# Loading a quad's queries and keys with one transfer over 120 partitions instead of two over 60, with a new rule table

## The chip, the cores and the metric

The kernel runs on one core of a Trainium2 chip. The metric is the device time of one execution in microseconds (us); the time before is the median of three runs. A profile of one further execution is shown beside it; its times are those of that one execution.

## The reference, cut to what matters

Two attention layers A and B with the same input `x` (2048 tokens of 640 numbers) and different weights are mixed by a gate per token. Each has 32 heads of 20 numbers, and the tokens are cut into 4 segments of 512.

```python
q, k, v = x @ wq, x @ wk, x @ wv                  # per head 20 numbers
for s in range(4):                                # segments of 512 tokens
    logits = einsum("hqd,hkd->hqk", qs, ks) * scale + mask
    a_dot  = softmax(logits) @ vs
    a_mem  = (phi(qs) @ M) / (phi(qs) @ z + 1e-6)
    o      = g * a_mem + (1 - g) * a_dot          # g = sigmoid(beta), per head
    M, z   = M + phi(ks).T @ vs, z + phi(ks).sum()
out = gate * (oA @ woA) + (1 - gate) * (oB @ woB) # gate per token
```

The mask takes out the keys that stand after the query, so that about half of the scores of a segment count.

## The kernel before, in words

One pass over eight windows `t` (segment `t // 2` of layer `t % 2`). In each window the projections q, k and v are made for 128 rows of the weights at a time. A product is kept near fp32 by splitting both sides into a high and a low part and adding three of the four products (line 819 for all of them but the first two and the last). The high and low parts of q and k are written to DRAM tensors `qd` and `kd` (line 798), three rows for each number of a head: (high, low, high) for q and (high, high, low) for k, so that one multiply over 3 x 20 = 60 rows gives the three products at once.

**Quads.** Attention works on a quad: four heads, as two pairs beside each other along the free axis and two halves of the array along the partitions. There are 64 quads, 8 in each window. `load_quads` reads a quad back from `qd` and `kd` into one of four buffers `qst` and one of four `kst` (line 1240): each is 128 partitions of 2 x 512 numbers, and half 0 has its 60 rows at partitions 0 to 59, half 1 at 64 to 123. That takes four transfers of 240 KB, two for q and two for k. A buffer is free when the quad four before it has had its second pass of scores (`t_over`).

**Two passes of scores.** `s_unit` multiplies q by k (line 1284) to find each query's largest score; VectorE takes the maximum out of PSUM with the triangle mask (line 1269), and the maxima `mx` are split in two parts, turned (line 1315), copied to a tile `mr` (line 1310) and sent by DMA into two spare rows of `qst` (line 1327). The matching rows of `kst` hold -1, so that `t_unit`, which multiplies k by q over 62 rows (line 1376), gives scores less their maximum. ScalarE takes the exponential into `p` (line 1368), GpSimd clears the half that is masked (line 1369), and `pv_unit` multiplies `p` with v (line 1396). The results go to DRAM tensors `dots`, come back (line 1517), are weighed by the inverse denominators (lines 1508 and 1509), turned, split (lines 1499, 1501 and 1502) and multiplied with `wo`, whose mixed form `wmix` is read through the buffers `wst` (line 567), as the other weights are. The memory `M` is updated in line 1030 and read in line 930.

**What sets the order.** The whole order is made when the kernel is built: a planner holds a clock for each half of TensorE and for each engine ("A", "D", "G" for ScalarE, VectorE, GpSimd, and "S" for SyncE, which issues all DMAs), with a cost in microseconds for each piece of work, and records the instructions in the order in which its model would do them. `dma(us, ...)` queues a transfer of `us` on a model of the DMA engines with at most 8 in flight. `put("D", 0.24, ...)` queues 0.24 us on VectorE; `anyof` gives a piece of work to the engine with the least queued. For each quad, a line of `RULES` sets in which order first ("S") and second ("T") passes stand, how they spread over the quad's time, and when work that may come late is let in. On the chip each engine takes its instructions strictly in the recorded order.

Of the kernel before, what the change touches and what calls it, by code (L numbers as in the profile page):

```python
# [42 lines left out]
def tile_gated_mix_infini_attn(  # L43
# [47 lines left out]
        0: "TTSSTTSSTS 1.01 2.38 0.22 8 0 1.6 1",  # L91
        1: "STTSTSSTST 1.021 2.38 0.4 4 0 1.6 1",
        2: "STSTSTSTST 0.96 2.38 0.3 8 0 1.6 1",
        3: "TTSTSTSTSS 0.967 2.38 0.33 8 0 2.23 1",
        4: "TTSSTTSSTS 1.028 2.22 0.3 8 0 1.6 1",
        5: "STSTSTSTST 1.01 2.38 0.38 8 0 2.37 1.15",
        6: "STTSTSSTST 1.01 2.38 0.3 8 0 1.6 1",
        7: "TSTTSSTSTS 0.96 2.11 0.27 8 0 1.6 1",
        8: "SSTSTSTSTT 1.013 1.26 0.3 8 0 1.6 1",
        9: "STTSTSSTST 1.01 2.38 0.28 8 0 1.6 1.33",  # L100
        10: "STTSTSSTST 1.01 2.38 0.3 8 0 1.6 1",
        11: "TSSTTSSTTS 1.077 1.88 0.3 8 0 1.6 1",
        12: "TSSTTSSTTS 1.01 2.38 0.3 8 0 2.97 1",
        13: "STTSTSSTST 1.01 1.86 0.23 8 0 1.31 0.39",
        14: "TSTSTSTSTS 1.01 2.38 0.3 8 0 1.6 1",
        15: "TTTSSTSTSS 1.01 2.38 0.3 8 0 1.6 1",
        16: "TTTSTSTSSS 0.996 2.38 0.3 8 0 1.6 1",
        17: "TTSTSTSTSS 1.01 3.27 0.3 8 0 1.6 1",
        18: "TTTSTSTSSS 1.01 2.38 0.3 8 0 1.6 1",
        19: "STSTSTSTST 1.01 2.38 0.32 8 0 1.6 1",  # L110
        20: "TSTSTSTSTS 1.01 2.38 0.28 0 0 1.6 1",
        21: "TSTSTSTSTS 0.985 2.38 0.3 8 3.8 1.6 1",
        22: "STSTSTSTST 1.013 2.38 0.37 0 1.4 1.6 1",
        23: "TSTSTSTSTS 1.01 2.38 0.3 4 0 1.6 1",
        24: "TSTSTSTSTS 1.065 2.38 0.36 8 0 1.8 1.23",
        25: "TTSSTTSSTS 1.01 2.38 0.3 8 0 1.6 1.84",
        26: "STSTTSTSTS 1.01 1.41 0.24 8 0 1.6 0.35",
        27: "SSTSTSTSTT 1.01 3.14 0.3 8 0 1.6 1",
        28: "TSTSTSTSTS 0.97 2.38 0.3 2 0 1.6 1",
        29: "TSTSTSTSTS 1.01 2.38 0.38 8 0 1.6 1",  # L120
        30: "STSTSTSTST 1.005 1.99 0.39 10 0 2.01 1.44",
        31: "TSTTSSTSTS 1.01 2.38 0.3 8 0 1.6 1",
        32: "SSTSTSTSTT 1.01 2.38 0.3 8 0 1.6 1",
        33: "TTTSSTSTSS 1.01 2.38 0.3 8 0 1.6 1",
        34: "TSTSTSTSTS 1.01 2.38 0.3 8 0 1.6 1",
# [1738 lines left out]
```

## Time and profile before the change

| what | before |
|---|---|
| median of 3 runs | 981.89 us (981.54 to 986.23) |
| the profiled execution, its own time | 985.52 us |
| its span, first to last instruction | 983.8 us |
| VectorE busy | 718.6 us (73%) |
| ScalarE busy | 671.4 us (68%) |
| GpSimd busy | 622.0 us (63%) |
| DMA moved | 236.02 MB, mean 240 GB/s |
| issues of 240 KB for `qst` and `kst` | 128 and 128 |

The busy share of an engine is an average over the whole span. For a multiply the profile shows when the array worked on anything at all: while one half of the array multiplies and the other waits, TensorE still counts as busy, so its share cannot show such a loss. "DMA share" in a window is the mean busy share of the 16 DMA engines; since packets overlap the window's ends it can stand a little over 1. "The chain" is the chain of work that ended last, followed back from the last instruction to what released each step; the releasers are inferred.

### The profile page before, as it was taken

The page shows a single profiled execution, that of the slowest core. Times are in us where ns is not written, and L with a number is a line of the kernel's source. Part 1 is how long each engine was busy: PE and PEld are TensorE (multiplying, and loading weights), DVE is VectorE, ACT ScalarE, POOL GpSimd, SP SyncE. Part 2 cuts the span into 40 slices and gives each one's busy share as a digit, 9 for nine tenths or more (in the row PEclk, how much of TensorE's full clock was granted, in tenths as well). Part 3 has the DMA queues.
Part 4 walks back from the last instruction along what each step waited for, and adds up shares of the span by engine and source line. Part 5 has one row for each costly group of instructions (what it writes and reads, how often), then busy time and mean ns, then how long its engine had stood idle before and what let it go on. Part 6 is the DMA issues. An engine that isn't in the chain of part 4 may idle for free.

```text
span 983.8 us, 31697 instructions
## 1 busy us (share of the span) xinstructions
PE 970.6 (99%) x11559; PEld 823.3 (84%) x11559; DVE 718.6 (73%) x2629; ACT 671.4 (68%) x1425; POOL 622.0 (63%) x1167
## 2 busy tenths in 40 slices
PE   9999999999999999999999999999999999999998
PEld 6987888888888888889788988797788888888876
DVE  4687966667788875887677968758666788678864
ACT  4378667677876676767686657876676667677572
POOL 4357558576557765767665677677584576658662
PEclk9999999999999999999999999999999999999999
DMA  6998988978888876887779777888675988779441
GB/s 212 306 314 233 304 256 300 311 225 253 261 288 236 296 223 189 297 259 232 208 219 286 233 222 221 236 276 249 201 229 175 283 263 265 233 228 275 115 128 54
DMA packets 148469, 236.02 MB, mean 240 GB/s; under 512 B 13173, under 2 KB 48794, under 8 KB 147994
## 3 DMA queue, kind: packets, MB, share of 16 engines
q1 hardware_dynamic: 148314, 234.00, 77.1%
q8 instruction: 91, 1.49, 0.7%
q14 instruction: 64, 0.52, 0.2%
HBM read 144.35 MB, written 95.11 MB: 243 GB/s over the span
## 4 chain that ended last, share of the span: by engine, by line
PE 91%; DMA 5%; issue 1%; DVE 1%; ACT 1%; SPq 1%; POOL 0%; ACTq 0%; POOLq 0%
PE bank L819 52%; PE bank L1396 15%; PE bank L1284 9%; PE bank L1376 8%; PE bank L930 3%; PE bank L972 2%; DMA wst<-in_a_wk_dram 2%; PE bank L1030 1%; DMA qst<-qd 1%; DMA kd<-row 1%; PE bank L869 1%; DMA kst<-kd 1%; DMA row<-dots 1%; PE bank L1211 0%; POOL wl L556 0%
## 5 line engine op out<-in xcount | busy, mean ns | idle before, releaser
L819 PE MATMUL bank<-row,wh 64*128 64x512 f32 x2308 | 479.5, 399 | 0.1
L1368 ACT ACTIVATE p<-bank 128x512 f32<-128x512 f32 x538 | 293.8, 601 | 101.9 <-PE bank L1376 84.6
L1269 DVE CUSTOM_DVE_ANT_0 junk<-bank,tri 128x128 bf16<-128x128 f32 (+2 forms) x768 | 279.5, 420 | 76.5 <-PE bank L1284 58.1
L819 PEld LDWEIGHTS bank<-row,wh 64*128 64x128 f32 x2308 | 315.8, 186 | 14.5 <-PE bank L819 1.1
L819 PE MATMUL bank<-row,wl 64*128 64x512 f32 x1154 | 293.6, 396 | 0.0
L1369 POOL TENSOR_SCALAR_AFFINE_SELECT p<-p 128x256 f32<-128x256 f32 (+1 forms) x538 | 195.0, 374 | 154.2 <-ACT p L1368 142.5
L556 POOL TENSOR_TENSOR wl<-wst,wh 128x640 fp32r<-128x640 f32 x115 | 180.4, 1574 | 64.7 <-ACT wh L558 46.0
L1269 DVE CUSTOM_DVE_ANT_0 bank<-bank,tri 128x512 f32<-128x512 f32 x256 | 172.6, 710 | 44.3 <-PE bank L1284 38.6
L819 PEld LDWEIGHTS bank<-row,wl 64*128 64x128 f32 x1154 | 176.4, 186 | 6.9 <-issue 0.8
L1284 PE MATMUL bank<-kst,qst 60*128 60x128 f32 (+3 forms) x1024 | 179.0, 329 | 2.4 <-ACT row L1499 1.3
L819 PE MATMUL bank<-wvh,row 64*128 64x320 f32 (+1 forms) x1280 | 172.8, 311 | 0.0
L1376 PE MATMUL bank<-qst,kst 62*128 62x128 f32 (+3 forms) x1024 | 170.4, 316 | 1.2 <-DVE row L1575 1.0
L819 PEld LDWEIGHTS bank<-wvh,row 64*128 64x128 f32 x1280 | 147.1, 186 | 2.2 <-PE bank L819 0.7
L1284 PEld LDWEIGHTS bank<-kst,qst 60*128 60x128 f32 x1024 | 129.0, 186 | 11.4 <-issue 2.0
L1376 PEld LDWEIGHTS bank<-qst,kst 62*128 62x128 f32 x1024 | 128.4, 186 | 10.9 <-issue 2.4
L1396 PE MATMUL bank<-p,vst 128*32 128x128 f32 (+3 forms) x1788 | 136.7, 425 | 0.0
L1396 PEld LDWEIGHTS bank<-p,vst 128*32 128x32 f32 x1788 | 55.6, 110 | 78.4 <-issue 55.7
L558 ACT CAST wh<-wst 128x640 fp32r<-128x640 f32 x119 | 86.1, 732 | 29.4 <-PE bank L819 14.0
L819 PE MATMUL bank<-wvl,row 64*128 64x320 f32 (+1 forms) x640 | 101.4, 310 | 0.0
L1269 DVE DVE_READ_ACCUMULATOR2_ANT mx<- 128x1 f32 x1024 | 100.0, 98 | 0.0
L819 PEld LDWEIGHTS bank<-wvl,row 64*128 64x128 f32 x640 | 82.1, 186 | 0.6 <-issue 0.4
L531 POOL TENSOR_TENSOR wvl<-wst,wvh 128x640 fp32r<-128x640 f32 (+1 forms) x48 | 60.0, 1254 | 16.1 <-DMA wst<-in_a_wv_dram 8.3
(122 smaller groups left out, 1160.4 us busy)
## 6 DMA issues: line engine op xcount, KB each, us to landing
qst<-qd SPq DMA_DIRECT2D x128, 240.0 KB
kst<-kd SPq DMA_DIRECT2D x128, 240.0 KB
qd<-row SPq DMA_DIRECT2D x40, 512.0 KB
kd<-row SPq DMA_DIRECT2D x40, 512.0 KB
dots<-row SPq DMA_DIRECT2D x56, 256.0 KB
wst<-wmix SPq DMA_DIRECT2D x35, 320.0 KB
qd<-row SPq DMA_DIRECT2D x40, 256.0 KB
kd<-row SPq DMA_DIRECT2D x40, 256.0 KB
```

Source lines behind the costliest of these rows:

```text
L531: put("G", 0.77 * n, lambda: nc.gpsimd.tensor_tensor(out=wl[:, a:b, :VN], in0=w3, in1=r32(wh[:, a:b, :VN]), op=ALU.subtract), end, prio=4)
L556: put(lo_eng, lo_cost, lambda: lo.tensor_tensor(out=wl, in0=w3, in1=r32(wh), op=ALU.subtract), end, prio=3)
L558: put("A", 0.625, lambda: nc.scalar.copy(wh, w3), low, prio=6)
L819: return nc.tensor.matmul(bank_of, lhsT=w[ROWS[half]], rhs=x_[ROWS[half]], start=start, stop=stop)
L930: return nc.tensor.matmul(pm[:, a - h0:c - h0, :].rearrange("p h e -> p (h e)"), lhsT=r32(pqTs[t, m][ROWS[half], P * n:P * (n + 1)]), rhs= ...
L972: return nc.tensor.transpose(px[:, n, r], block(n)[r], ident[r, r])
L1269: nc.vector.tensor_tensor_reduce(out=sc[:, off:off + w] if w == L else junk[:, at_:at_ + w], in0=sc[:, off:off + w], in1=tri[:, L - w:], s ...
L1284: lane_ops[half].append((mm(w), lambda pair=pair, qb=qb, off=off, w=w, r=r, sc=sc: nc.tensor.matmul(sc[:, off:off + w], lhsT=q[r, pair, P ...
L1368: put("A", 0.483, lambda: nc.scalar.activation(pt, sc, AF.Exp, scale=SCALE), lambda: (bank.give(sc), put("G", 0.15 + 0.105 * len(todo), la ...
L1369: "G", 0.15 + 0.105 * len(todo), lambda: nc.gpsimd.affine_select(out=blocks, in_=blocks, pattern=[[0, len(todo)], [1, P]], base=0, channel ...
L1376: lane_ops[half].append((mm(w), lambda pair=pair, kb=kb, off=off, w=w, r=r, sc=sc: nc.tensor.matmul(sc[:, off:off + w], lhsT=k[r, pair, P ...
L1396: nc.tensor.matmul(po[32 * j:32 * j + 32, P * kb:], lhsT=vst[t % 2][:, kb, h * E1:h * E1 + 32], rhs=pts[i, n, f][0][:, off:off + w], start ...
```

## The change

The rows of half 0 move from partitions 0 to 59 to partitions 4 to 63, so that with half 1 at 64 to 123 a quad fills 120 neighbouring partitions, and one transfer of 480 KB brings q and one k. Partitions 0 to 3 of `qst` then take part in the first pass for half 0 (64 rows instead of 60): they must be zero there, since the same partitions of `kst` hold -1. A DRAM tensor `zeros` is filled once from the cleared `qst[0]`, and a third transfer for each quad copies 16 KB of it over those four partitions. The maxima of half 0 now go to partitions 0 and 1, those of half 1 to 124 and 125, and the second pass takes partitions 0 to 63 and 64 to 125. The planner's costs change with it: 1.35 for a transfer of 480 KB instead of 0.95 for one of 240 KB, 0.05 for the zeros, 0.69 or 0.62 for the maxima of a unit instead of 0.763 or 0.638, and 0.14 instead of 0.24 for the turn. All 66 lines of `RULES` are new.

```diff
     RULES = {
-        0: "TTSSTTSSTS 1.01 2.38 0.22 8 0 1.6 1",
+        0: "TSTSTSTSTS 1.01 2.38 0.29 8 0 0.91 1",
...
+    zeros = dram.tile([4, 2, L], F32, name="zeros")
...
-        while next_load[0] < 64:
+        while next_load[0] < 64 and zeros_there:
...
-            done = then_all(4, lambda i=i: loaded.add(i))
-            r0, soon = 80 * u, marks[i - LEAD] if i >= LEAD else -2
+            done = then_all(3, lambda i=i: loaded.add(i))
+            r0, soon, lat = 80 * u, marks[i - LEAD] if i >= LEAD else -2, 0.9 if i > 1 else 2.8
             for dst, src in ((q, qd[t]), (k, kd[t])):
-                rows = src[r0:r0 + 80, :, :].rearrange("(p f d) c n -> f (d c) p n", p=2, f=2)
-                for half in range(2):
-                    dma(0.95, lambda dst=dst, src=rows[half], half=half: nc.sync.dma_start(
-                        out=r32(dst[64 * half:64 * half + 3 * DH, :, :]), in_=r32(src)), done, prio=soon, lat=0.9 if i > 1 else 2.8)
+                rows = src[r0:r0 + 80, :, :].rearrange("(p f d) c n -> (f d c) p n", p=2, f=2)
+                dma(1.35, lambda dst=dst, src=rows: nc.sync.dma_start(
+                    out=r32(dst[4:4 + 6 * DH, :, :]), in_=r32(src)), done, prio=soon, lat=lat)
+            dma(0.05, lambda q=q: nc.sync.dma_start(out=r32(q[:4, :, :]), in_=zeros), done, prio=soon, lat=lat)
...
-            r = slice(64 * half, 64 * half + 60)
+            r = slice(64, 124) if half else slice(0, 64)
...
-                put("D", sum(P * (qb + 1) for _, qb, _ in todo) / 960.0 + 0.125 * len(todo) - 0.02, both,
+                put("D", 0.69 if len(todo) > 1 else 0.62, both,
...
-        put("D", 0.24, lambda: turn_rows(i), lambda: mr_store.want(1, lambda mr: move_rows(i, mr), prio=0), prio=1)
+        put("D", 0.14, lambda: turn_rows(i), lambda: mr_store.want(1, lambda mr: move_rows(i, mr), prio=0), prio=1)
...
-            r = 64 * half + 60
+            r = 124 * half
...
-            r = slice(64 * half, 64 * half + 62)
+            r = slice(64, 126) if half else slice(0, 64)
...
+    at(9.0, lambda: dma(0.05, lambda: nc.sync.dma_start(
+        out=zeros, in_=r32(qst[0][:4, :1, :]).to_broadcast([4, 2, L])), lambda: (zeros_there.append(1), load_quads()), prio=-3))
```

What this moves on the engines is seen in the recorded order. A row is one instruction: line, operation, what it writes, what it reads, the shape written, and how many of the same follow each other. Line numbers of the code behind the new tensor are mostly one higher after the change.

SyncE's queue at the load of the first quad (`qst_80`, `kst_84`), before:

```order
L567 DMA wst_150<-in_a_wq_dram 128x640
L567 DMA wst_151<-in_a_wk_dram 128x640
L1240 DMA qst_80<-qd_97 60x2x512 x2
L1240 DMA kst_84<-kd_105 60x2x512 x2
L798 DMA qd_97<-row_249_384 128x2x512
L798 DMA qd_97<-row_250_385 128x512
```

and after:

```order
L568 DMA wst_152<-in_a_wk_dram 128x640
L1240 DMA qst_80<-qd_97 120x2x512
L1240 DMA kst_84<-kd_105 120x2x512
L1242 DMA qst_80<-zeros 4x1024
L799 DMA qd_97<-row_252_386 128x2x512
L799 DMA qd_97<-row_253_387 128x512
```

Four transfers have become three, at the same place between the weights and the next writes to `qd`.

SyncE's queue at the load of quad 11 (`qst_83`, `kst_87` out of `qd_98` and `kd_106`), in the second window, before; `inv` holds the inverse denominators and `dots` the results of a window:

```order
L1442 DMA dots_118<-row_3034_2944 128x512
L798 DMA kd_106<-row_3025_2937 128x2x512
L798 DMA kd_106<-row_3026_2938 128x512
L1465 DMA row_2826_2766<-inv_124 128x1x512
L1517 DMA row_3057_2969<-dots_117 128x1x512
L567 DMA wst_151<-wmix_137 128x5x128
L567 DMA wst_150<-wmix_137 128x5x128
L1240 DMA qst_83<-qd_98 60x2x512 x2
L1240 DMA kst_87<-kd_106 60x2x512 x2
L1240 DMA qst_80<-qd_98 60x2x512 x2
L1240 DMA kst_84<-kd_106 60x2x512 x2
```

and after:

```order
L1328 DMA qst_80<-mr_168 2x8x128 x2
L1443 DMA dots_117<-row_2456_2496 128x512
L1240 DMA qst_83<-qd_98 120x2x512
L1240 DMA kst_87<-kd_106 120x2x512
L1242 DMA qst_83<-zeros 4x1024
L539 DMA wst_151<-in_b_wv_dram 128x320
L799 DMA kd_106<-row_2572_2596 128x2x512
L799 DMA kd_106<-row_2573_2597 128x512
L568 DMA wst_150<-in_a_wk_dram 128x640
L1328 DMA qst_81<-mr_168 2x8x128 x2
```

Before, this load stood behind the way back of the first window's results and the mixed weights, with the next quad's load right behind it; after, it stands ahead of the last value weights of its window, ahead of all of those.

TensorE's queue ahead of the first quad's first scores, before:

```order
L819 MATMUL bank_144<-wvh,row_72_230 128x322
L819 MATMUL bank_141<-wvh,row_67_227 128x322
L819 MATMUL bank_144<-wvl,row_13_200 128x322
L819 MATMUL bank_141<-wvh,row_72_230 128x322
L819 MATMUL bank_144<-wvl,row_20_202 128x322
L819 MATMUL bank_141<-wvl,row_13_200 128x322
L819 MATMUL bank_144<-wvl,row_25_204 128x322
L1284 MATMUL bank_143<-kst_84,qst_80 128x512
```

and after:

```order
L820 MATMUL bank_142<-wvh,row_25_205 128x322
L820 MATMUL bank_145<-wvh,row_25_205 128x322
L820 MATMUL bank_142<-wvh,row_67_227 128x322
L820 MATMUL bank_145<-wvh,row_67_227 128x322
L820 MATMUL bank_142<-wvh,row_72_230 128x322
L1285 MATMUL bank_146<-kst_84,qst_80 128x512
```

The first scores are asked for earlier: 214 rows of the order stand ahead of them before, 200 after, and the low parts (`wvl`) of these two banks of the value product have moved behind them or far ahead. Over the whole program TensorE has the same multiplies in both; VectorE has 7 more of the subtractions and products over a whole row that `anyof` hands out (lines 1501 and 1508 before: 12 and 18, after the change 15 and 22), GpSimd 7 fewer (lines 1502 and 1509 before: 23 and 17, after 20 and 13).

More of the change, by code (lines that the diff above doesn't have):

```diff
@@ L1220, in quad @@
         return t, u, qst[i % NQ], kst[i % NQ]
-    loaded, next_load, t_over = set(), [0], set()
+    loaded, next_load, t_over, zeros_there = set(), [0], set(), []
     def load_quads():
-        while next_load[0] < 64:
+        while next_load[0] < 64 and zeros_there:
             i = next_load[0]
```

130 rows, old and new, of the table RULES are left out of this document.

## The prediction

> **What bounds the kernel now.** I read the head of the page and the shares of the chain first.
>
> ```profile
> span 983.8 us, 31697 instructions
> PE 970.6 (99%) x11559; PEld 823.3 (84%) x11559; DVE 718.6 (73%) x2629; ACT 671.4 (68%) x1425; POOL 622.0 (63%) x1167
> PE 91%; DMA 5%; issue 1%; DVE 1%; ACT 1%; SPq 1%; POOL 0%; ACTq 0%; POOLq 0%
> q1 hardware_dynamic: 148314, 234.00, 77.1%
> ```
>
> TensorE works 970.6 of 983.8 us, so it stands still for 13.2 us in all, and 91% of the chain is its own work. No other engine is full. The only other resource with a share worth a look is the DMA engines: 77.1% of their time, and 5% of the chain, about 49 us. Next the long pieces of the chain, in order of time (start, length, what), without those of TensorE:
>
> ```profile
> 21.11 9.61 DMA qst<-qd
> 30.78 8.25 DMA wst<-in_a_wk_dram
> 41.32 7.61 DMA wst<-in_a_wk_dram
> 175.35 6.69 DMA kst<-kd
> 658.92 5.19 DMA row<-dots
> 672.19 6.76 DMA kd<-row
> 704.18 2.28 issue
> ```
>
> Two of the pieces are loads of a quad, the thing that is changed: the first at 21 us, and one at 175 us. Then the busy times by window (start:end, length, then TensorE, its weight loads, VectorE, ScalarE, GpSimd with their counts, the granted clock, the DMA share and GB/s):
>
> ```profile
> 0.00:60.00 60.00, 57.07 (x482) 49.19 (x484) 37.26 (x122) 30.78 (x69) 25.34 (x46) 1.00 0.85 273
> 170.00:172.00 2.00, 2.00 (x30) 1.97 (x28) 0.00 (x0) 0.70 (x2) 1.85 (x2) 1.00 1.05 405
> 175.00:182.00 7.00, 7.00 (x75) 7.00 (x73) 5.26 (x5) 3.77 (x7) 4.71 (x3) 1.00 1.03 261
> 182.00:186.00 4.00, 2.67 (x21) 2.04 (x19) 2.59 (x5) 3.19 (x8) 2.47 (x3) 1.00 1.07 227
> 182.00:188.00 6.00, 4.67 (x38) 4.04 (x36) 4.59 (x7) 4.80 (x10) 4.07 (x6) 1.00 1.09 250
> 300.00:655.00 355.00, 354.64 (x4328) 302.15 (x4322) 267.44 (x951) 251.17 (x529) 239.73 (x434) 1.00 0.79 243
> 909.00:912.00 3.00, 3.00 (x45) 2.02 (x38) 2.50 (x9) 2.65 (x7) 3.00 (x4) 1.00 1.00 222
> 914.20:915.20 1.00, 1.00 (x19) 1.00 (x17) 0.96 (x5) 0.81 (x2) 0.82 (x4) 1.00 0.00 0
> ```
>
> The clock is 1.00 throughout. At 170 to 172 us, where transfers over 128 partitions run, full DMA engines move 405 GB/s. At 182 to 188 and at 909 to 912, with little in flight but loads of quads, engines that are just as busy move 250 and 222. So a load over 60 partitions keeps the engines busy for longer than its bytes need. That is the room this change has. How much of it is on the path is another matter, and the waits of TensorE (waiting line, what released it, us in total, times, longest) with the rows of its first scores in time order show it:
>
> ```profile
> PE bank L1284 <- ACT row L1499: 1.3, 1, 1.3
> PE bank L1376 <- DVE row L1575: 1.0, 1, 1.0
> PE bank L1284 <- ACT p L1368: 0.8, 1, 0.8
> 185.17 0.60 PE L1284 MATMUL bank<-kst,qst 60*128 60x512 f32 x2 [1.33 <-ACT row L1499]
> L1284 PE MATMUL bank<-kst,qst x176: 217/370/494, 32.9 to 158.1; 60*128 60x512 f32 x44, 60*128 60x128 f32 x44, 60*128 60x384 f32 x44, 60*128 60x256 f32 x44
> L1284 PE MATMUL bank<-kst,qst x992: 217/382/502, 32.9 to 921.6; 60*128 60x128 f32 x52, 60*128 60x512 f32 x51, 60*128 60x256 f32 x49, 60*128 60x384 f32 x47
> 926.99 0.65 PE L1284 MATMUL bank<-kst,qst 60*128 60x512 f32 x2
> 173.74 1.11 SPq L1240 DMA_DIRECT2D qst<-qd  x2
> 906.32 0.80 SPq L1240 DMA_DIRECT2D qst<-qd  x2
> ```
>
> A quad has 16 first-pass multiplies, so the 176 before 185 us are those of quads 0 to 10, and the one at 185.17 opens quad 11, whose load was issued at 173.74. TensorE stood still for 1.33 us ahead of it, and the DMA engines were full all the way. The 992 before 926.95 us are quads 0 to 61: quad 62 opens at 926.99, its load was issued at 906.32, and at 914.2 the DMA engines are empty. This load was there some 12 us too early. Both kinds exist, and a faster load is worth something in the first kind only.
>
> **The loads themselves.** A quad is 4 x 240 KB, 0.983 MB. At 250 GB/s that is 3.9 us, at 222 it is 4.4, at 405 it is 2.4. The trace has no load over 120 partitions: its bounds are 3.9 us (no faster) and 2.4 us (as fast as the row at 170 us). I take 2.7, since 120 neighbouring partitions are nearer to 128 than to 60. That saves 1.2 us for each quad and 77 us of DMA time over 64, and takes the DMA share from 77% to about 69%. On the path:
> - Around quad 11, 21 multiplies run in the 4 us from 182 against 75 in the 7 us before, which is 5.3 for each us against 10.7: half the work is missing, 2.0 us. The recorded order also puts this load ahead of the way back of the first window. I count **-2.0**; between 0 and -3.
> - In the first 60 us TensorE stands still for 2.9 us, of which the start of the program is the greater part, while the chain runs through three DMAs (9.61, 8.25 and 7.61 us). Three quads' loads, each 1.2 us shorter, bring what queues behind them 1 to 3.6 us forward; the value products of the window cover most of that. **-1.5**; between 0 and -4.
> - At 659 and 672 us the chain goes through `dots` and `kd`, and TensorE stands still 1.0 and 0.8 us there. Transfers that share the engines with shorter loads land sooner: **-0.5**; between 0 and -2.
> - The other loads are hidden as quad 62's is: **0**.
>
> [...]
>
> **What is added.** SyncE issues three transfers for a quad where it issued four.
>
> ```profile
> L1240 SPq DMA_DIRECT2D qst<-qd x128: 319/396/2036, 20.7 to 918.6; - x128
> L1240 SPq DMA_DIRECT2D kst<-kd x128: 315/417/1748, 22.4 to 919.6; - x128
> L1327 SPq DMA_DIRECT2D qst<-mr x128: 610/622/1134, 43.6 to 952.0; - x128
> SPq L1240 <- PE bank L1376: 76.3, 31, 8.2
> ```
>
> At some 0.4 us an issue (the middle number is the median in ns) the 64 fewer issues free 26 us of SyncE. It waits in other places: 76.3 us in all for the second pass that frees a buffer. So **0**; between -2 and 0. The zeros are 64 x 16 KB, 1 MB beside 236, nothing as bytes. But S now has to wait for them, and they are issued last. The nearest row is the small transfer of the maxima, 0.62 us of issue. Where the load has 12 us to spare this is hidden; on a late quad it eats at most one issue: **0**; up to +2 if it happens on three quads. The one transfer that fills `zeros` is asked for at 9 us of the plan, and the first load is issued at 20.7 us; this gap covers it. If it did not, the first load would slip.
>
> The first pass of half 0 takes 64 rows of the array instead of 60, and the second pass 64 or 62:
>
> ```profile
> L819 PE MATMUL bank<-row,wh 64*128 64x512 f32 x2308 | 479.5, 399 | 0.1
> L1284 PE MATMUL bank<-kst,qst 60*128 60x512 f32 x256 | 69.5, 407 | 1.5 <-ACT row L1499 1.3
> L1376 PE MATMUL bank<-qst,kst 62*128 62x512 f32 x256 | 66.9, 411 | 0.0
> ```
>
> 60, 62 and 64 rows by 512 columns take 407, 411 and 399 ns: rows cost nothing, **0**, with no gain or loss to expect, since the counts are the same.
>
> **The new order.** Here the trace gives bounds only. Seven subtractions and products go from GpSimd to VectorE:
>
> ```profile
> L1502 POOL TENSOR_TENSOR row<-row,row 128x512 fp32r<-128x512 f32 x23 | 30.5, 1341 | 7.8 <-ACT row L1499 6.2 <-DMA qd<-row 1.4 <-POOL p L1369 0.2
> L1501 DVE TENSOR_TENSOR row<-row,row 128x512 fp32r<-128x512 f32 x12 | 13.7, 1158 | 3.0 <-ACT row L1499 2.1 <-DMA qd<-row 1.0
> ```
>
> At 1.34 and 1.16 us that is 9 us off GpSimd and 8 us onto VectorE, which is busy 73%: hidden, 0. What a new table of rules can win is the standstill that is left, 13.2 us less the 3.1 of quad 11 and the two later waits, and some of the half-array losses that busy time cannot show. What it can lose are places like the ones above: each costs 1 to 2.3 us, and a handful of new ones is +8. I take -8 to +8, and inside this **-3**: the costs that the planner uses for the loads drop by 1.05 us a quad, near the 1.2 that I expect of the chip, so that its order should fit the chip no worse than before, and it has 67 us less of DMA time to work around.
>
> **The sum.** -2.0 - 1.5 - 0.5 - 3 = -7.0 us. The profiled execution took 985.5 us by its own time, 983.8 of span and 1.7 around it; it would come to 978.5, a ratio of 0.993. The median of the runs, 981.9, is 0.4% lower than that execution; the same ratio gives **975 us**.
>
> **The rivals.**
> - *Hidden anyway* (chance 0.27). Quad 62's 12 us to spare is the rule, quad 11 the exception, and TensorE is full at 354.64 of 355 us in the middle of the program. Then the loads give 2 to 3 us and the table nothing: 979 to 980 us. For it speaks the stretch from 300 to 655; against it the start, where DMA is the chain.
> - *The DMA engines were the hidden brake* (0.13). If DMA lateness holds halves of the array in many places where busy time does not show it, 77 us less DMA work is worth more: a third of the 49 us of DMA in the chain, 16 us, with the table's 3 on top: 963 us. For it: share 0.85 and above up to 200 us. Against it: the middle.
> - *The load does not get faster, and the plan counts on it* (0.17, slower). If 120 partitions still move at 250 GB/s, q and k take 3.9 us and not the planned 2.7, and each load lands 1.2 us later than the order expects. In the first 200 us, where the DMA share is 0.85 to 1.03, there are 13 loads; if half of these are late like quad 11's, that is 8 us, and with the zeros' +2 the profiled time is 995 and the median about 991. It decides from the point where a load is issued less than its own time ahead of its first scores. In the queue, the quads that are read at the end of a window, right behind the writes to `kd`, are the ones to be hit.
> - *The table opens new standstills* (0.08, no change to slower): up to +8 on the -4 of the loads, 986 us.
>
> [...] No row here shows which engines a transfer used; the 405 GB/s against 250 at equal busy share speak for slow packets instead of missing engines.
>
> **How the numbers follow.** The forecast has 0.35, with its own range 970 to 979. Within 0.5% (4.9 us, about what a measurement of this kernel can tell from no change) is 977 to 987; faster is below, slower above. Faster takes the second rival and nearly all of the forecast, and a part of the first where the table helps: 0.13 + 0.32 + 0.09 = 0.54. Slower takes the third and a part of the fourth: 0.17 + 0.03 = 0.20. The rest is 0.26. The range leaves out the far ends of the second and third rival: 961 to 990.
>
> **What would show it.** Loads alone in flight move over 330 GB/s at full DMA share, and the DMA share falls below 72%: the transfers are right. No wait of a first score above 1 us between 170 and 200 us: quad 11 is right. The DMA pieces of the chain up to 50 us fall below 20 us in sum: the start is right. If GB/s stays at 250 with loads alone, the third rival holds. If TensorE stands still for over 13 us in places that this trace doesn't have, it is the table. The forecast is wrong if the loads get faster and TensorE's standstill and the time stay as they are.

## The result and the profile after

The changed kernel takes 1011.9 us (median of four runs, 1007.56 to 1017.48) against 982.1: a ratio of 1.0297, 95% interval 1.0239 to 1.0356. It is slower by some 30 us where 7 us less were forecast, and it lies outside the forecast's 961 to 990 us. The profiled execution took 1012.82 us.

The head of the page after the change, with the shares of the chain and the DMA queue:

```profile
span 1011.1 us, 31575 instructions
PE 983.5 (97%) x11559; PEld 833.4 (82%) x11559; DVE 717.3 (71%) x2630; ACT 674.4 (67%) x1431; POOL 616.8 (61%) x1160
PE 74%; DMA 16%; ACT 3%; SPq 2%; DVE 2%; POOL 2%; issue 1%; POOLq 0%; ACTq 0%; DVEq 0%
q1 hardware_dynamic: 146918, 235.06, 77.0%
```

TensorE stands still for 27.6 us instead of 13.2, DMA has 16% of the chain instead of 5%, and the DMA queue is busy for 77.0% of a longer span: the 69% that faster loads would have left did not come. But TensorE is also *busy* for 12.9 us more with the same number of multiplies, 11559. The span and the mean granted clock of the core tell why, first for the changed kernel, then for the kernel before:

```profile
core 0: 1011.1 us, clock 0.989
```

```profile
core 0: 983.8 us, clock 0.999
```

A mean of 0.989 over 1011.1 us is 11 us of clock not granted, against 1 us before. So some 14 of the 27 us of span are standstill and some 10 are a slower clock; what the last 3 are is not shown. The windows of the changed kernel (start:end, length, busy time of TensorE, weight loads, VectorE, ScalarE, GpSimd, clock, DMA share, GB/s) show that a slower clock follows some of the standstills:

```profile
0.00:60.00 60.00, 53.59 (x431) 46.47 (x433) 33.87 (x108) 28.15 (x63) 24.29 (x43) 0.97 0.83 252
184.00:188.00 4.00, 1.75 (x22) 1.48 (x19) 0.00 (x0) 0.00 (x0) 2.76 (x4) 1.00 1.00 324
188.00:192.00 4.00, 1.97 (x13) 1.86 (x15) 1.28 (x3) 2.57 (x7) 0.29 (x1) 0.86 1.00 228
192.00:196.00 4.00, 4.00 (x31) 4.00 (x29) 2.37 (x8) 2.85 (x7) 3.29 (x3) 0.71 0.67 195
300.00:655.00 355.00, 349.31 (x4217) 297.64 (x4215) 255.53 (x931) 246.13 (x518) 228.99 (x420) 0.99 0.79 233
708.00:712.00 4.00, 4.00 (x39) 4.00 (x38) 2.84 (x10) 1.27 (x3) 2.16 (x2) 0.50 0.72 212
928.00:934.00 6.00, 3.95 (x61) 3.75 (x58) 4.66 (x13) 0.63 (x2) 3.65 (x3) 1.00 1.01 226
934.00:940.00 6.00, 6.00 (x71) 5.66 (x67) 5.03 (x26) 0.85 (x2) 0.00 (x0) 1.00 1.06 237
```

From 184 to 192 TensorE works 3.72 of 8 us, and then, fully busy, only at a clock of 0.71: 31 multiplies in 4 us. At 708 to 712 the clock is 0.50. The trace's record of the clock has five such stretches at 0.50 ahead of the last multiply, 20.5 us together, and half of that is the 10 us. In the middle, 300 to 655, TensorE stood still for 0.4 us before and now for 5.7. The windows from 928 to 940 hold three quads' loads nearly alone (three weight transfers join them in the second), at full DMA share: 226 and 237 GB/s. **The wide load is as slow as the narrow ones were.** Next come the waits of TensorE (waiting line, what released it, us in total, times, longest), and long pieces of the chain without TensorE's own (start, length, what):

```profile
PE bank L1285 <- DMA kst<-kd: 6.3, 5, 2.1
PE bank L1285 <- ACT row L1428: 4.3, 1, 4.3
PE bank L1285 <- DMA qst<-zeros: 1.6, 2, 0.9
```

```profile
19.89 6.50 DMA wst<-in_a_wq_dram
31.31 8.27 DMA wst<-in_a_wk_dram
39.64 11.03 DMA wst<-in_a_wk_dram
177.62 11.68 DMA kd<-row
425.66 10.20 DMA kst<-kd
674.89 8.49 DMA kst<-kd
694.81 9.04 DMA kd<-row
```

Before, first scores waited for a late load in no row of this list; now they do so seven times, 7.9 us. And the longest pieces are not only loads of quads but also what queues behind them: the write to `kd` at 177.62 takes 11.68 us to land, ScalarE's next `row` waits for it (the 4.3 us of the second row), and TensorE for that.

### The profile page after: what moved, and what is told of

It is laid out like the page before. It is cut to its first block, busy times and chain, and to the rows that moved or that the text cites. A ratio compares the mean times of both kernels' runs of the same rounds, so it can differ in the third digit from the quotient of the medians.

```text
span 1011.1 us, 31575 instructions
## 1 busy us (share of the span) xinstructions
PE 983.5 (97%) x11559; PEld 833.4 (82%) x11559; DVE 717.3 (71%) x2630; ACT 674.4 (67%) x1431; POOL 616.8 (61%) x1160
## 4 chain that ended last, share of the span: by engine, by line
PE 74%; DMA 16%; ACT 3%; SPq 2%; DVE 2%; POOL 2%; issue 1%; POOLq 0%; ACTq 0%; DVEq 0%
PE bank L820 42%; PE bank L1397 11%; PE bank L1285 8%; PE bank L1377 6%; DMA kst<-kd 4%; DMA kd<-row 3%; PE bank L931 3%; DMA wst<-in_a_wk_dram 2%; PE bank L973 2%; DMA qd<-row 2%; DMA qst<-zeros 1%; DMA dots<-row 1%; PE bank L1031 1%; ACT p L1369 1%; DMA row<-dots 1%
## 5 line engine op out<-in xcount | busy, mean ns | idle before, releaser
L820 PE MATMUL bank<-row,wh 64*128 64x512 f32 x2308 | 505.1, 402 | 1.9 <-ACT mr L716 1.8
L820 PEld LDWEIGHTS bank<-row,wh 64*128 64x128 f32 x2308 | 327.5, 187 | 14.4 <-ACT mr L716 2.2
L820 PE MATMUL bank<-row,wl 64*128 64x512 f32 x1154 | 307.5, 399 | 0.1
L1285 PE MATMUL bank<-kst,qst 64*128 64x384 f32 (+7 forms) x1024 | 179.7, 332 | 15.4 <-DMA kst<-kd 6.3
L820 PE MATMUL bank<-wvh,row 64*128 64x320 f32 (+1 forms) x1280 | 190.1, 312 | 0.0
L1377 PE MATMUL bank<-qst,kst 62*128 62x512 f32 (+7 forms) x1024 | 170.6, 315 | 0.9 <-ACT p L1369 0.5
L820 PEld LDWEIGHTS bank<-wvh,row 64*128 64x128 f32 x1280 | 159.0, 185 | 2.5 <-issue 1.0
L1285 PEld LDWEIGHTS bank<-kst,qst 64*128 64x128 f32 (+1 forms) x1024 | 128.6, 186 | 29.7 <-issue 7.2
L1397 PE MATMUL bank<-p,vst 128*32 128x384 f32 (+3 forms) x1816 | 140.5, 423 | 0.0
L1377 PEld LDWEIGHTS bank<-qst,kst 62*128 62x128 f32 (+1 forms) x1024 | 129.7, 185 | 9.0 <-ACT p L1369 1.5
```

Source lines behind the costliest of these rows:

```text
L820: return nc.tensor.matmul(bank_of, lhsT=w[ROWS[half]], rhs=x_[ROWS[half]], start=start, stop=stop)
L1285: lane_ops[half].append((mm(w), lambda pair=pair, qb=qb, off=off, w=w, r=r, sc=sc: nc.tensor.matmul(sc[:, off:off + w], lhsT=q[r, pair, P ...
L1377: lane_ops[half].append((mm(w), lambda pair=pair, kb=kb, off=off, w=w, r=r, sc=sc: nc.tensor.matmul(sc[:, off:off + w], lhsT=k[r, pair, P ...
L1397: nc.tensor.matmul(po[32 * j:32 * j + 32, P * kb:], lhsT=vst[t % 2][:, kb, h * E1:h * E1 + 32], rhs=pts[i, n, f][0][:, off:off + w], start ...
```

## The experiments

Each ratio is to the kernel before on the same chip, with its 95% interval in brackets; a "point" is 0.01 of such a ratio. "Old order" is the order, costs and rules of before; "new order" those of the change. "Narrow" is two transfers over 60 partitions, "wide" one over 120. A line of three dots in a diff stands for lines left out.

### Transfers alone (e1, e9)

Kernels of nothing but transfers, eight or sixteen of a kind behind one another.

```diff
+    def rows_120_at_4():
+        for j in range(NT):
+            nc.sync.dma_start(out=ts[j][4:124, :, :], in_=src(j, 120))
...
```

> Only transfers, no attention: eight phases of eight loads of one quad's size each, the phases kept apart, and then the output is a copy of the transposed input. In order: two halves of 60 partitions; 120 partitions from 4 on; 120 from 0 on; 128; 112; 64; 120 from 4 on with one 240 KB transfer for each pair; and the same 120 rows from DRAM to DRAM. Theory A (the load over 120 partitions is as slow as two over 60, and the place in SBUF that is written decides it): the first three phases and the pair by pair one move 220 to 260 GB/s at full DMA share, 128 partitions about 400, 64 about 220, DRAM to DRAM well above 260. Theory B (the way the rows are read decides it): DRAM to DRAM is at 220 to 260 too. Theory C (120 is fast and the whole kernel's mixed traffic slowed it): the second phase moves over 330.

Windows of this run inside six of the stretches: two narrow, wide at 4, 128 partitions, 112, over 120 partitions but one pair (240 KB) at a time, and the same 120 rows from DRAM to DRAM:

```profile
6.00:20.00 14.00, 3.65 (x10) 0.00 (x0) 1.00 1.00 216
25.00:40.00 15.00, 0.92 (x6) 0.00 (x0) 1.00 1.00 222
65.00:75.00 10.00, 1.07 (x7) 0.00 (x0) 1.00 1.02 377
80.00:90.00 10.00, 0.77 (x5) 0.00 (x0) 1.00 1.04 270
108.00:120.00 12.00, 1.08 (x7) 0.00 (x0) 1.00 1.00 260
122.00:124.00 2.00, 0.51 (x14) 0.00 (x0) 1.00 0.98 381
```

The last number is GB/s, ahead of it the DMA share. 120 partitions move 222, narrow 216: hardly faster. 128 move 377. The same bytes cut by pairs move 260. From DRAM to DRAM the same rows move 381, so it is the place that is written and not the reading that makes them slow: theory A.

The second run of this kind has other widths, and quads' loads mixed with other transfers (`gap`: four of 256 KB over 128 partitions):

```diff
+    def mix_wide():
+        for i in range(NQ):
+            for j in (2 * i, 2 * i + 1):
+                nc.sync.dma_start(out=ts[j][4:124, :, :], in_=src(j % 8, 120))
+            gap(i)
...
```

> Only transfers, in seven stretches one after the other; the output is the input. First eight loads each over 104, 126 and 96 partitions, then ten rounds of a quad's q and k followed by four transfers of 256 KB over 128 partitions, with q and k as before (60 partitions at 0 and at 64), narrow (at 4 and at 64), wide (120 at 4) and over 128. [...]

```profile
6.00:18.00 12.00, 10.22 (x12) 0.00 (x0) 1.00 0.86 218
58.00:70.00 12.00, 0.92 (x6) 0.00 (x0) 1.00 0.93 276
85.00:95.00 10.00, 0.92 (x6) 0.00 (x0) 1.00 1.07 254
112.00:180.00 68.00, 2.61 (x17) 0.00 (x0) 1.00 1.03 277
195.00:265.00 70.00, 2.61 (x17) 0.00 (x0) 1.00 0.98 253
285.00:350.00 65.00, 2.77 (x18) 0.00 (x0) 1.00 1.03 280
365.00:410.00 45.00, 2.30 (x15) 0.00 (x0) 1.00 1.05 385
```

The rows are 104, 126 and 96 partitions, then the four mixes with 128-partition transfers: as before, narrow at 4, wide, 128. 104 partitions move 218, at a DMA share of 0.86, and 96 move 254. 126 move 276, at a share of 0.93, over the 222 of 120 and far under the 377 of 128, and among transfers over 128 partitions the wide loads do *not* slow their neighbours (280 against 277). The narrow loads at 4 and 64, which cost nothing in the old order further down (e7), are the slowest here (253). Of all widths tried only 128 partitions come near 380 (377 in e1, 385 in the last mix). So whatever a wide load costs in the kernel more than a narrow one is not its mean rate in a steady row.

### Does the wish for a fast load explain the loss (e5, e3, e10, e11)?

```diff
-                dma(1.35, lambda dst=dst, src=rows: nc.sync.dma_start(
-                    out=r32(dst[4:4 + 6 * DH, :, :]), in_=r32(src)), done, prio=soon, lat=lat)
+                if i >= NQ:
+                    a = max(0, 3 * r0 - 16)
+                    rows = src.rearrange("d c n -> (d c) n")[a:a + 2 * P, :].rearrange("(p r) n -> r p n", p=2)
+                dma(1.35, lambda dst=dst, src=rows, g=slice(0, P) if i >= NQ else slice(4, 124): nc.sync.dma_start(
+                    out=r32(dst[g, :, :]), in_=r32(src)), done, prio=soon, lat=lat)
```

> The order of the changed kernel, but from the fifth quad on q and k come in transfers over all 128 partitions (512 KB instead of 480 KB, rows of neighbours where the spare rows were, so the scores' values are not the reference's) and without the zeros. Alone, such transfers moved 354 GB/s against 220 over 120 partitions. Theory A (the new order is sound, it only counts on loads of 2.7 us and gets 4.2): the wish of the plan comes true, DMA share under 70%, few late first scores, time at or under that of the kernel before, 0.985 to 1.000 of it. Theory B (the new order itself costs, whatever the loads do): 1.005 or more, as with half the bytes (1.0026) or worse. Theory D (a wide transfer hurts because it is one and not two): above 1.015.

1.0058 (1.0025 to 1.009), just inside theory B. Truly fast loads repair most of the loss, and the DMA share comes down about as far as I had forecast for the change:

```profile
q1 hardware_dynamic: 148478, 238.01, 71.6%
```

But the kernel is not faster than before: the 5.5 points of DMA share win nothing, and the new order costs a little.

```diff
+                n = 2 if i < NQ else 1
...
-                    out=r32(dst[4:4 + 6 * DH, :, :]), in_=r32(src)), done, prio=soon, lat=lat)
+                    out=r32(dst[4:4 + 6 * DH, :n, :]), in_=r32(src[:, :n, :])), done, prio=soon, lat=lat)
```

> The changed kernel's order, with only the first pair of each quad loaded from the fifth quad on (240 KB instead of 480, the second pair keeps older numbers; the attention of these pairs is not computed). At some 240 GB/s a transfer then takes 1.0 us, less than the 1.35 of the plan. Theory A (loads later than the plan): most of the loss of 30 us goes, 978 to 992, no half clock behind quads 12, 28, 37 and 46, since what the plan counts on is there. Theory E (the new order is bad for another reason, the engines' costs or the table): at least 1000.

1.0026 (0.9997 to 1.0055), with a DMA share of 64.6%: as theory A expected, and the same answer.

```diff
-                dma(1.35, lambda dst=dst, src=rows: nc.sync.dma_start(
+                dma(2.1, lambda dst=dst, src=rows: nc.sync.dma_start(
```

> The changed kernel, rules and all, with one number changed: the planner counts 2.1 instead of 1.35 for each wide transfer, 4.2 us a quad, which is what the chip takes. Theory A (the loss is the plan's too short load): 1.015 of before or less. Theory D (wide transfers cost in themselves, through what they do to the transfers beside them): 1.015 to 1.03, near the changed kernel's 1.029. Since the order is made anew, a chance of 0.5% either way remains.

1.1139 (1.1093 to 1.1185). With the true cost in the plan the kernel is eleven points slower than before, and over eight slower than with the short one. The next run is the changed kernel with the rules of before:

```diff
-        0: "TSTSTSTSTS 1.01 2.38 0.29 8 0 0.91 1",
+        0: "TTSSTTSSTS 1.01 2.38 0.22 8 0 1.6 1",
...
```

> The changed kernel with the 66 lines of rules of before; loads, zeros and planner's costs are those of the change. Theory B (the new lines of rules carry the loss): 1.005 of before or less. Theories A and D (the loads do): 1.008 to 1.03.

1.0631 (1.0592 to 1.0671). Both miss what every theory expected, and on the same side. Rules and costs are fitted to each other; a cost in this planner is a setting, not a measurement, and a change of one number says little about the load. The "too short cost" is neither shown to be the cause nor ruled out by these two.

### One wide transfer or two narrow ones (e2, e4, e7, e8)

```diff
-                dma(1.35, lambda dst=dst, src=rows: nc.sync.dma_start(
-                    out=r32(dst[4:4 + 6 * DH, :, :]), in_=r32(src)), done, prio=soon, lat=lat)
+                dma(1.35, lambda dst=dst, src=rows: [nc.sync.dma_start(
+                    out=r32(dst[4 + 60 * h:64 + 60 * h, :, :]), in_=r32(src[60 * h:60 * h + 60])) for h in range(2)],
...
```

> The changed kernel's order, layout and zeros, but each transfer of 480 KB issued as two of 60 partitions in the same place of the queue. Theory A (the shape of the transfer is worth nothing, the new order counts on a speed that is not there): within 6 us of the changed kernel, 1006 to 1018. Theory D (the wide transfer itself hurts, by holding one of the eight places in flight for longer or by blocking others): clearly faster, under 1000.

1.0093 (1.0074 to 1.0111), against the changed kernel measured again beside later runs:

> The changed kernel once more, for a comparison on the same chip as the other runs: 1.024 to 1.036 of before by its first measurement.

1.0288 (1.0251 to 1.0325). The order of every engine is the same, the bytes are the same, the place in the queue is the same: cutting each wide transfer in two brings back two thirds of the loss. The old order shows it too. Before's kernel with the new layout, zeros and wide loads, each in the place of its first half:

```diff
...
                 for half in range(2):
...
+                    def emit(dst=dst, src=rows, half=half, zero=zero, q=q):
+                        if half == 0:
+                            nc.sync.dma_start(out=r32(dst[4:4 + 6 * DH, :, :]), in_=r32(src))
+                        elif zero:
+                            nc.sync.dma_start(out=r32(q[:4, :, :]), in_=zeros)
...
```

> The order of the kernel before, with its costs and table, but the new layout: the wide transfer for q in the place of its first half, for k in the place of its first half, the zeros in the place of the last one. Theory A: the same as before, 978 to 988, since the transfer is neither better nor worse. Theory D: slower than 990. What I had predicted of the transfer (2.7 us for a quad): 975 to 980.

1.0084 (1.0056 to 1.0112), as theory D expected. And with narrow loads (the lines that differ from the run just shown):

```diff
-                            nc.sync.dma_start(out=r32(dst[4:4 + 6 * DH, :, :]), in_=r32(src))
+                        nc.sync.dma_start(out=r32(dst[4 + 60 * half:64 + 60 * half, :, :]), in_=r32(src[60 * half:60 * half + 60]))
...
```

> The order, costs and rules of before with the new layout and the zeros, but each q and k in two transfers over 60 partitions (4 to 63 and 64 to 123), the zeros behind the last of them. Against the run with wide transfers in this same order (0.8% slower than before) it differs in nothing but the width. Theory D (the width itself costs): within 0.3% of before. Theory Z (zeros, and rows at 4 to 63): 0.6 to 1.0% slower, as with wide transfers.

0.9987 (0.9961 to 1.0013). Layout, 64 rows and zeros cost nothing there; the wide transfer costs one per cent. One place where it does is shown by the same windows of the wide run, with a piece of its chain, and then of the narrow one.

```profile
650.00:656.00 6.00, 6.00 (x79) 5.96 (x77) 2.98 (x6) 4.75 (x11) 6.00 (x5) 1.00 0.97 249
656.00:662.00 6.00, 3.81 (x45) 3.33 (x43) 2.67 (x10) 3.22 (x9) 1.08 (x5) 1.00 0.56 181
```

```profile
652.35 7.89 DMA qd<-row
```

```profile
650.00:656.00 6.00, 6.00 (x81) 5.96 (x79) 3.43 (x7) 5.64 (x12) 5.75 (x8) 1.00 0.94 270
656.00:662.00 6.00, 6.00 (x67) 5.18 (x65) 4.91 (x21) 4.01 (x9) 3.01 (x6) 1.00 0.83 219
```

Behind the wide q and k the write to `qd` lands after 7.89 us. In the narrow run the same write lands after 3.84 us (its issue at 652.60, the last increment of its semaphore at 656.44). (In the trace of the kernel before, all 160 writes to `qd` and `kd` and 254 of the 256 loads of quads show 16 increments of their semaphore, the other two loads 15; the last is taken as the landing.) Of the late write 15 increments were there after 5.4 us, and the last came 2.5 us behind them, while the mean DMA share fell to 0.56. The quads themselves hardly land later: over 64 quads the mean from the first issue to the last k is 8.5 us wide and 8.4 narrow. It is the transfers behind them that do. The same reading for all writes to `qd` and `kd`, some 160 in each run:

| loads | order | mean from issue to landing | writes over 8 us |
|---|---|---|---|
| kernel before | old | 5.0 us | 0 |
| wide (e4) | old | 5.5 us | 12 |
| narrow (e7) | old | 5.1 us | 0 |
| wide (changed kernel) | new | 5.3 us | 8 |
| narrow (e2) | new | 5.0 us | 2 |

A last increment that lags is not a mark of wide loads, though: over these writes it comes 0.4 to 0.5 us behind the one before it in all five, and from 173.7 to 180.8 us of the kernel before eight loads of 240 KB in a row have one that is 1.9 to 2.5 us late.

### The zeros (e6, e15, e16)

```diff
-            dma(0.05, lambda q=q: nc.sync.dma_start(out=r32(q[:4, :, :]), in_=zeros), done, prio=soon, lat=lat)
+            dma(0.05, lambda q=q, i=i: nc.sync.dma_start(out=r32(q[:4, :, :]), in_=zeros) if i < NQ else None, done, prio=soon, lat=lat)
```

> The changed kernel with the zeros copied only for the first four quads (later quads hold old maxima in two of these rows, so the values of half 0 change); the order of all other work is the same. Theory Z (each quad waits for the zeros, issued last, landing 6.3 us after their issue against 5.6 and 7.0 of q and k): 5 us or more below the changed kernel on this chip. Theories A and D: the k transfer lands last anyway, within 3 us of the changed kernel.

1.0215 (1.018 to 1.0251), 0.7 points or 7 us under the changed kernel. The same edit for the wide loads in the old order, and for the narrow ones in the new order:

> Before's order with wide transfers, zeros only for the first four quads. If the width alone costs: 1.006 to 1.011 of before, as with zeros. If the zeros behind the wide k are what is late: 0.997 to 1.003.

1.0071 (1.0044 to 1.0098), about as with zeros (1.0084).

> The changed kernel's order with two transfers over 60 partitions in the place of each wide one, zeros only for the first four quads: as much data as before, moved as slowly as before, in the new order. If the new order itself costs (the run with 128 partitions: 1.003 to 1.009): 1.003 to 1.009. If half of what the narrow run lost (1.009) is the zeros': 1.000 to 1.005.

1.0086 (1.0053 to 1.0119), as with zeros (1.0093). In these runs the zeros cost only where wide loads and the new order already make first scores late.

### Smaller pieces (e13, e14, e17, e18, e12)

```diff
-                dma(1.35, lambda dst=dst, src=rows: nc.sync.dma_start(
-                    out=r32(dst[4:4 + 6 * DH, :, :]), in_=r32(src)), done, prio=soon, lat=lat)
+                dma(1.35, lambda dst=dst, src=rows: [nc.sync.dma_start(
+                    out=r32(dst[4:4 + 6 * DH, p, :]), in_=r32(src[:, p, :])) for p in range(2)],
+                    done, prio=soon, lat=lat)
```

> The changed kernel's order with each transfer of 480 KB cut in two by pairs: 240 KB each, each over all 120 partitions; alone such pieces moved 261 GB/s against 220 uncut and 213 cut into halves of 60 partitions. Theory G (the size of the piece: one engine that is behind with 16 packets of a transfer holds back all that queues behind it): like the narrow cut, 1.005 to 1.012 of before. Theory S (the span: with 120 partitions the engines hinder each other and the slowest one lags): like the changed kernel, 1.02 or more.

1.0028 (1.0002 to 1.0054): all but 0.3 points of the loss is gone, with every piece still over 120 partitions. That is better than either theory expected, and it speaks against theory S. The hole that stood at 186 to 190 us is smaller. This run is some 3 us earlier here, so its window is 180 to 184, and its wait ahead of the same first scores, after ScalarE's same `row`, is 1.06 us instead of 4.28:

```profile
180.00:184.00 4.00, 2.94 (x40) 2.52 (x33) 0.66 (x2) 0.91 (x4) 3.72 (x6) 1.00 1.00 348
```

```profile
PE bank L1286 <- ACT row L1429: 1.1, 1, 1.1
```

The write to `kd` at this place lands after 7.6 us instead of 11.7. The same cut in the old order (the lines that differ from e7):

```diff
-                        nc.sync.dma_start(out=r32(dst[4 + 60 * half:64 + 60 * half, :, :]), in_=r32(src[60 * half:60 * half + 60]))
+                        nc.sync.dma_start(out=r32(dst[4:124, half, :]), in_=r32(src[:, half, :]))
...
```

> Before's order with the new layout and the zeros, each of the four transfers of a quad over 120 partitions and one pair. Theory G: as with 60 partitions in this order, 0.996 to 1.002 of before. Theory S: as with wide transfers in this order, 1.006 to 1.011.

0.994 (0.9916 to 0.9963): **this version is faster than both kernels**, by some 6 us than the one before, and again better than either theory expected. From its page:

```profile
span 977.8 us, 31866 instructions
PE 968.1 (99%) x11559; PEld 826.3 (85%) x11559; DVE 715.0 (73%) x2629; ACT 671.5 (69%) x1425; POOL 622.7 (64%) x1167
PE 96%; DMA 2%; POOL 1%; DVE 1%; ACT 0%; issue 0%; SPq 0%; DVEq 0%; ACTq 0%
q1 hardware_dynamic: 148838, 235.07, 75.8%
```

DMA has 2% of the chain instead of 5%. Without the zeros it gets no better:

> Before's order with q and k pair by pair over 120 partitions as in the run that took 0.994 of before, and zeros only for the first four quads (the softmax takes out what old maxima add). If the zeros cost nothing where loads are early: 0.991 to 0.997 of before, the same as with them. If they hold back first scores: 0.985 to 0.991.

0.996 (0.9939 to 0.9982), as with them. Next, narrow transfers cut once more, to 120 KB (the lines that differ from e7):

```diff
-                        nc.sync.dma_start(out=r32(dst[4 + 60 * half:64 + 60 * half, :, :]), in_=r32(src[60 * half:60 * half + 60]))
+                        for p in range(2):
+                            nc.sync.dma_start(out=r32(dst[4 + 60 * half:64 + 60 * half, p, :]), in_=r32(src[60 * half:60 * half + 60, p, :]))
...
```

> Before's order with the new layout and the zeros; each transfer over 60 partitions cut by pairs into two of 120 KB, eight for a quad. SyncE has 256 issues more, some 100 us, of which it has as much in waits. Theory G (the size of the piece alone): the narrow run's 0.999 or less, down to the 0.994 of the pairs. Theory V (the speed of the pairs over 120 partitions, 261 GB/s alone, made their gain, and size counts only between 480 and 240 KB): 0.997 to 1.003, as narrow. Issues: 1.003 or more if SyncE is late.

1.0101 (1.0068 to 1.0135), worse than narrow (0.9987). The chain of this run and of the narrow one:

```profile
PE 83%; DMA 9%; SPq 3%; ACT 2%; issue 1%; DVE 1%; POOL 0%; ACTq 0%; DVEq 0%
```

```profile
PE 91%; DMA 6%; DVE 1%; SPq 1%; ACT 1%; issue 1%; POOL 0%; ACTq 0%; DVEq 0%
```

SyncE's queue now stands in the chain with 3%. So "smaller is better" does not hold for the time. It does for the landings: the writes to `qd` and `kd` take 4.7 us on the mean, less than with narrow loads (5.1) or pairs (e14, 4.8), and none takes over 8. What the run loses it loses elsewhere; the eight issues for a quad are the likely reason, not shown alone. Last, q in two transfers over all 128 partitions (for 48 quads), k narrow:

```diff
...
+                            a = 240 * u + 120 * half - 4
+                            nc.sync.dma_start(out=r32(dst[:, half, :]), in_=r32(qd[t].rearrange("d c n -> (d c) n")[a:a + P, :]))
...
```

> Before's order, costs and rules; k in two transfers over 60 partitions as in the narrow run; q of a quad in two transfers of 256 KB over all 128 partitions, one for each pair, wherever four rows of neighbours stand on both sides (48 of 64 quads), and no zeros from the fifth quad on: what stands in the spare rows adds the same number to all scores of a query, which the softmax takes out again. [...] If lateness of transfers is what costs before's order its last per cent, 0.99 to 0.997 of before; if not, 0.997 to 1.003.

1.0007 (0.9983 to 1.003), with a DMA share of 76.3% against 78.6 in e7: faster bytes, no time. Together with e5 and e3 this says that less work for the DMA engines, alone, makes neither order faster than the kernel before.

The six runs that share zeros and layout, with nothing but the order and the pieces of q and k between them:

| pieces | old order | new order |
|---|---|---|
| two of 240 KB over 60 partitions | 0.9987 (e7) | 1.0093 (e2) |
| one of 480 KB over 120 | 1.0084 (e4) | 1.0288 (e8) |
| two of 240 KB over 120, by pairs | 0.994 (e14) | 1.0028 (e13) |

## Why the prediction was wrong

**The loads.** The step that failed first is "I take 2.7, since 120 neighbouring partitions are nearer to 128 than to 60". A wide q and k take 960 KB at 222 GB/s, 4.4 us, a little over the bound "no faster" of 3.9. That bound came from 182 to 188 us, where mixed weights and writes to `qd` were in flight too; the row of 222 at 909 to 912, where only quads were loaded, was the better one. The 77 us of DMA time were never there (share 77.0%). In the traces, for 60 and for 120 partitions alike, one of a load's 16 increments comes early and 15 come with the data. The medians are 0.57 us after the issue for q and 0.60 for k in the kernel before, with the next increment after 3.24 and 4.10 us, and 0.52 and 0.61 in the changed one, with the next after 4.04 and 5.75. For the writes of 128 rows to `qd` and `kd`, in the kernel before, the median of the first is 3.03 and 3.35 us. What the early increment stands for, and so which engines a load used, no run shows. Nor does the rate grow with the width, as I had taken it to: 112 partitions move 270 GB/s and 120 move 222 (e1).

**On the path.** -2.0 at quad 11, -1.5 in the first 60 us and -0.5 at 659 became losses at the same places: the wait of 1.33 us at 185 (quad 11's) is one of 4.28 us at 190 (now that of quad 12, by the count of first scores), the standstill of the first 60 us from 2.9 to 6.4, and the pieces at 675 and 695 take 8.5 and 9.0 us. The places were read rightly, as those where DMA decides: in the kernel before, the last increment of quad 11's k comes at 185.04 us, 0.13 us ahead of its first scores, though the page names ScalarE's `row` for the wait. The sign was wrong.

**What I had no term for**: at equal bytes and nearly equal rate, one piece of 480 KB costs more than two of 240. It is 0.97 points in the old order (e4 against e7), 1.95 in the new one (e8 against e2), and 2.6 against pieces that are also faster (e8 against e13). The prediction treated a transfer as bytes over a rate and asked only when *it* lands; what stood in the queue behind it paid, and that it had put at nothing without a reason.

**What is added.** No run tests SyncE's issues alone; its queue has 2% of the chain after the change and 1% before, so no gain is seen. For the rows of the array 0 holds: 417 ns over 60 rows and 411 over 64 in the changed kernel.

```profile
L1285 PE MATMUL bank<-kst,qst 60*128 60x512 f32 x128 | 53.2, 417 | 10.7 <-DMA kst<-kd 6.0 <-ACT row L1428 4.3 <-ACT row L1369 0.5
L1285 PE MATMUL bank<-kst,qst 64*128 64x512 f32 x128 | 52.6, 411 | 1.9 <-DMA qst<-zeros 1.6 <-DMA kst<-kd 0.3
```

The zeros were mis-sized: "0, up to +2" is right in e7 and e16, but in the changed kernel they are 7 us.

**The new order.** -3 was the wrong side of its own range, and the range was too small. With the same loads the new order costs 0.9 points by pairs (e13 against e14) and 1.1 with narrow loads (e2 against e7), some 9 to 10 us; with wide loads it is 2.0 (e8 against e4). So the loss of 2.9 points is about one of the order, one of the wide piece, and one that comes only when both meet.

**The rivals.** The third, "the load does not get faster", named the right fact and the right sign, and priced it at 991 us. Of the place it had the quads read behind the writes to `kd`; at 177 us the late one is a write to `kd` behind a quad's load. It was 21 us short. It counted half of 13 loads at 1.2 us each; it had no price for the transfers held up behind it, and none for the clock. Its other half, "the plan counts on it", is not needed for most of the loss: in e13 q and k take 3.8 us by the 260 GB/s of e1, an estimate, far over the planned 2.7, and 0.3 points are left. e10 does not bear it out either. The fourth, new standstills from the table, is the other part: up to 8 us, where the order costs 9 to 10 at equal loads.

**What stays open** is why a transfer behind a wide piece lands later. A last increment that lags does not explain it, since narrow loads have it too; and e9 shows that it takes more than loads beside 128-partition transfers in a steady row (280 GB/s with wide loads, 253 with narrow ones). Nor is it the bytes of a piece alone: those of e5 are larger, 512 KB, and cost no more than narrow ones without zeros (1.0058 against 1.0086 in e16). By the rates of e1, an estimate, such a piece holds the engines for 1.4 us and a wide one for 2.2. e2 and e7 keep the rate and change only the piece, so at that rate the piece has a part of its own; e13 makes pieces both smaller and faster (260 against 222), and e18 would part the two but loses time elsewhere.

## What to carry to other kernels

Price a merged transfer by a measured rate of its own shape, not between two neighbours, and then ask who stands behind it in the queue: here the merge left the rate nearly as it was (216 and 222 GB/s in e1) and the transfers behind it landed later (a write to `qd` after 7.89 us in e4 and 3.84 in e7). Before taking a cost out of a planner whose rules were fitted to it, change the transfer alone in the old order; here that run (e4) shows the loss, and its neighbour (e14, the same span in pieces of one pair) the gain. And a kernel that keeps TensorE full can pay twice for a standstill of a few us, as this one did, the second time by the clock after it: 14 us of standstill here and 10 us of clock.

## What the runs showed of the hardware that was not expected

- 120 and even 126 partitions move 222 and 276 GB/s where 128 move 377 (e1, e9). More partitions are not always faster: 96 move 254 (e9) and 112 move 270 (e1), both over the 222 of 120. Why is not shown.
- A transfer over 120 partitions with one run of 2 KB for each partition moves 260 GB/s, with two runs 222 (e1). In this kernel, too, the larger piece is the worse one in its effect (1.0288 against 1.0028).
- In the changed kernel the granted clock fell to 0.50 after five of the nine standstills of TensorE of over 1 us behind the first 10 us (1.56 us at 31, 4.28 at 186, 2.10 at 434, 1.04 at 573 and 1.26 at 704 us), though TensorE was busy again by then; after the other four (1.83 at 50, 1.62 at 314, 1.08 at 669 and 2.05 at 931) it did not, nor after 1.33 us at 184 and 2.28 at 704 in the kernel before. The five stretches last 3.41 us each, the last one 6.83, and begin at 33.89, 190.90, 436.66, 576.61 and 706.31 us: 46, 72, 41 and 38 steps of 3.413 us apart. So the clock seems to be set once in 3.41 us; which standstill lowers it is not shown. It cost 10 us here; in e14, with 9.7 us of standstill, the mean clock is 1.000.
